# Splitting the first weight load of a two-problem GQA kernel, and reordering its first matmuls around the two pieces

## The chip, the cores and the metric

The kernel runs on one core of a Trainium2 chip. The metric is device time in microseconds (us) from one launch.

Names used below: PE is TensorE, PEld its weight loads, DVE is VectorE, ACT is ScalarE, SP is the sync engine, which here issues almost all DMA loads. SPq or PEq in a profile is the sequencer of that engine, which waits and issues. Lnnn is a line of the kernel; lines after L485 are up to four higher in the changed kernel.

## The reference

Two independent problems A and B, each a block of grouped-query attention with cached keys and values; their outputs are put side by side.

```python
# per problem: x (16, 32, 1024), k/v cache (16, 4, 512, 128), wq (1024, 4096), wo (4096, 1024), bf16
q = (x @ wq).reshape(16, 32, 32, 128).transpose(0, 2, 1, 3)
k = jnp.repeat(k_cache, 8, axis=1); v = jnp.repeat(v_cache, 8, axis=1)
p = softmax(einsum("bhqd,bhkd->bhqk", q, k) * 128 ** -0.5)
o = einsum("bhqk,bhkd->bhqd", p, v).transpose(0, 2, 1, 3).reshape(16, 32, 4096) @ wo
```

## The kernel before

The program has a head and a long main loop. The head projects the first 8 query heads of problem A (`first_heads`), 8 chunks of 128 along the model dimension by 8 heads, into 8 accumulators that fill PSUM. Then 128 slots of attention follow (128 pairs of batch and key head); in each slot 7 (in every fourth 6) "units", that is background matmuls, are mixed in: the projections of all other heads of A, then those of B, then the output projections. This mixing keeps PE full.

The head, with cuts:

```python
NF = REP - 2          # 6 heads start first; REP = 8
HC = DC // 2          # DC = 8 chunks of the model dimension, TT = 4 blocks of 128 tokens
...
load_x(0, 0, TT // 2)             # tokens, chunks 0 and 1, first half of the tokens: 128 KB
load_w0(0, 1, 0, NF)              # weights of chunk 0, heads 0..5: 192 KB, rows of 1,536 bytes
load_x(0, TT // 2, TT)            # the other token half: 128 KB
load_w0(1, 2, 0, NF)              # weights of chunk 1: 192 KB
load_x(2, 0, TT)                  # tokens, chunks 2 and 3: 256 KB  ("second-chunk tokens" below)
load_w0(2, 3, 0, NF)
load_w0(3, 4, 0, NF)
load_w0(0, HC, NF, REP)           # heads 6 and 7, chunks 0..3: 256 KB
load_w0(HC, HC + 2, 0, REP)       # 512 KB
load_x_transposed(HC)             # tokens, chunks 4 and 5, transposed by the DMA: 256 KB
load_w0(HC + 2, DC, 0, REP)
load_x_transposed(HC + 2)
load_wq(0, 2)                     # weights of heads 8..11: 1 MB, the first of the streamed projections
load_k(0)
...
warm_up(22)                       # 128-column matmuls on constants, result not used
transpose_x(0, 0, TT // 2)        # PE transposes, then DVE copies one chunk and ACT the other
warm_up(2)
first_heads(range(0, NF // 2), (0,), 0, TT // 2)
transpose_x(0, TT // 2, TT)
first_heads(range(NF // 2, NF), (0,), 0, TT // 2)
first_heads(range(NF), (0,), TT // 2, TT)
first_heads(range(0, NF // 2), (1,))
transpose_x(2, 0, TT)             # the "second transposes"
first_heads(range(NF // 2, NF), (1,))
first_heads(range(NF), (2, 3))
...                               # heads 6 and 7, then chunks 4..7; results leave PSUM
```

The loads of the main loop are issued by SP from a plan, slot by slot. SP issues them in this one order, and each waits there for its buffer to be free:

```python
at(GRP * (j - 1) - 2, load_k, j)                            # keys, 4 slots' worth
at(GRP * (j - 1) + 2, load_v, j, 2 if j < 4 else 1)         # values
at(max(0, int(need) - 10), load_wq, c4 // 8, c4 % 8)        # 1 MB of projection weights
for n, (d0, d1) in enumerate(((0, 2), (2, 5), (5, DC))):    # tokens of problem B, DMA-transposed,
    at(GRP * (n + 4) - 2, load_xT_b, d0, d1)                # in three parts: slots 14, 18, 22
```

## Time and profile before

| | kernel before |
|---|---|
| time, median | 344.55 us (343.79 to 344.85, 3 executions) |
| span of the profiled execution | 342.3 us |
| PE busy | 335.6 us, 98% |
| first head matmul | 4.50 us |
| second transposes begin | 7.65 us |
| hand-over: first matmul of the streamed projection | 19.98 us |
| last output matmul starts | 338.94 us |

Two parts of the page of the kernel before, busy time by engine and the chain of waits that ended last:

```profile
PE 335.6 (98%) x2087; PEld 214.1 (63%) x2126; DVE 266.5 (78%) x336; ACT 186.1 (54%) x209; POOL 47.1 (14%) x206
PE 96%; DMA 1%; issue 1%; SPq 1%; ACT 0%; ACTq 0%
```

The timeline of PE in the head shows where it stands still. Columns: start in us, time to the end of the group in us (ends are modelled, so groups overlap), engine, line, operation, output and inputs, count, and in brackets idle time before it and what ended it.

```profile
3.24 0.63 PE L521 MATMUL xT_ps<-ident,x_sb 128*128 128x128 bf16 x4
3.67 0.42 PE L513 MATMUL q_ps<-const-bfloat16-1.0 128*128 128x128 bf16 x2
4.50 0.82 PE L531 MATMUL q_ps<-xT,w_sb 128*128 128x256 bf16 x3 [0.41 <-DMA w_sb<-in_A_wq_dram]
5.11 0.63 PE L521 MATMUL xT_ps<-ident,x_sb 128*128 128x128 bf16 x4
5.54 1.89 PE L531 MATMUL q_ps<-xT,w_sb 128*128 128x256 bf16 x12
7.65 0.62 PE L521 MATMUL xT_ps<-ident,x_sb 128*128 128x128 bf16 x8 [0.22 <-DMA x_sb<-in_A_x_dram]
8.33 11.82 PE L531 MATMUL q_ps<-xT,w_sb 128*128 128x512 bf16 x53
19.98 1.24 PE L302 MATMUL q_ps<-xT,wq_sb 128*128 128x512 bf16 x5
...
```

The brackets count from the modelled end of the matmul before. Measured from start to start, less what a matmul of that size takes in a dense stream (107 ns per 128 columns at first, later 56, 109 and 216 ns for 128, 256 and 512), PE lost 0.62 us before 4.50 us and 0.38 us before 7.65 us. All waits given below are counted in that second way. The 0.22 us hole before 8.33 us is a dropped record: its weight load is there.

### The profile page before, as it was taken

The page shows a single profiled execution, that of the slowest core. Times are in us where ns is not written, and L with a number is a line of the kernel's source. Part 1 is how long each engine was busy: PE and PEld are TensorE (multiplying, and loading weights), DVE is VectorE, ACT ScalarE, POOL GpSimd, SP SyncE. Part 2 cuts the span into 40 slices and gives each one's busy share as a digit, 9 for nine tenths or more (in the row PEclk, how much of TensorE's full clock was granted, in tenths as well). Part 3 has the DMA queues.
Part 4 walks back from the last instruction along what each step waited for, and adds up shares of the span by engine and source line. Part 5 has one row for each costly group of instructions (what it writes and reads, how often), then busy time and mean ns, then how long its engine had stood idle before and what let it go on. Part 6 is the DMA issues. An engine that isn't in the chain of part 4 may idle for free.

```text
span 342.3 us, 5465 instructions
## 1 busy us (share of the span) xinstructions
PE 335.6 (98%) x2087; PEld 214.1 (63%) x2126; DVE 266.5 (78%) x336; ACT 186.1 (54%) x209; POOL 47.1 (14%) x206
## 2 busy tenths in 40 slices
PE   8999999999999999999999999999999999999996
PEld 6456666666666666666666666666666666666555
DVE  1057988888889888988888888888988888888540
ACT  2067666676676666666655455555455445555010
POOL 0001111100111111111101112222122110111100
PEclk9999999999999999999999999999999999999999
DMA  6988999999899999999999457998449985440001
GB/s 186 313 218 192 334 249 262 259 213 243 243 255 251 273 247 241 223 254 285 261 333 279 138 124 194 291 313 223 117 119 300 333 188 139 105 112 0 17 17 33
DMA packets 126958, 71.70 MB, mean 209 GB/s; under 512 B 75857, under 2 KB 126161, under 8 KB 126929
## 3 DMA queue, kind: packets, MB, share of 16 engines
q1 hardware_dynamic: 126400, 70.21, 84.4%
q0 software_dynamic: 384, 1.05, 0.9%
q8 instruction: 17, 0.28, 0.3%
q14 instruction: 13, 0.10, 0.1%
q10 hardware_dynamic: 144, 0.07, 0.1%
HBM read 50.86 MB, written 2.10 MB: 155 GB/s over the span
## 4 chain that ended last, share of the span: by engine, by line
PE 96%; DMA 1%; issue 1%; SPq 1%; ACT 0%; ACTq 0%
PE f_ps L321 32%; PE q_ps L302 28%; PE ob L426 17%; PE s_ps L358 16%; PE q_ps L531 3%; DMA x_sb<-in_A_x_dram 1%; SPq L478 0%; SPq L466 0%; PE xT_ps L521 0%; ACT o_sb L330 0%; SPq L701 0%; ACTq L330 0%
## 5 line engine op out<-in xcount | busy, mean ns | idle before, releaser
L366 ACT ACTIVATE p_sb<-s_ps,shift 128x1024 bf16<-128x1024 f32 x128 | 142.7, 1115 | 100.0 <-PE s_ps L358 85.7
L377 DVE TRANSPOSE_TENSOR_REDUCE parts<-p_sb 128x32 f32<-128x1024 bf16 x128 | 158.9, 1241 | 19.4 <-ACT p_sb L366 17.9
L321 PE MATMUL f_ps<-wo_sb,oT 128*128 128x512 bf16 (+1 forms) x525 | 127.5, 366 | 0.6
L302 PE MATMUL q_ps<-xT,wq_sb 128*128 128x512 bf16 x430 | 113.7, 379 | 0.6
L426 PE MATMUL ob<-p_sb,v_sb 128*128 128x256 bf16 x512 | 76.8, 273 | 0.8
L358 PE MATMUL s_ps<-qT,kT 128*128 128x256 bf16 x512 | 76.8, 273 | 0.0
L321 PEld LDWEIGHTS <-oT 128*128 128x128 bf16 x544 | 53.2, 98 | 36.0
L358 PEld LDWEIGHTS <-kT 128*128 128x128 bf16 x512 | 56.8, 113 | 28.4 <-issue 0.3
L302 PEld LDWEIGHTS <-wq_sb 128*128 128x128 bf16 x448 | 43.8, 98 | 31.5
L426 PEld LDWEIGHTS <-v_sb 128*128 128x128 bf16 x512 | 50.1, 98 | 20.0
L448 DVE TENSOR_TENSOR oT<-r,ob 128x512 bf16<-128x512 f32 x64 | 44.0, 687 | 22.5 <-PE ob L426 22.0
L412 DVE STREAM_TRANSPOSE r<-rall 128x512 f32<-128x512 f32 x64 | 44.2, 691 | 1.1
L310 ACT CAST qT<-q_ps 128x512 bf16<-128x512 f32 x56 | 32.7, 583 | 13.8 <-PE q_ps L302 13.8
L395 POOL COPY half<-cs 64x32 f32<-64x32 f32 x32 | 6.6, 206 | 228.1 <-DVE cs L385 228.1
L330 ACT CAST o_sb<-f_ps 128x512 bf16<-128x512 f32 (+1 forms) x17 | 9.5, 559 | 24.4 <-PE f_ps L321 16.7
L531 PE MATMUL q_ps<-xT,w_sb 128*128 128x512 bf16 (+1 forms) x68 | 14.5, 368 | 0.5 <-DMA w_sb<-in_A_wq_dram 0.4
L385 DVE TENSOR_REDUCE cs<-parts 128x32 f32<-128x128 f32 x32 | 12.0, 376 | 1.1
L407 DVE RECIPROCAL rall<-sums 128x32 f32<-128x32 f32 x32 | 10.5, 329 | 1.7 <-POOL sums L404 1.6
L531 PEld LDWEIGHTS <-w_sb 128*128 128x128 bf16 x70 | 6.9, 101 | 7.2 <-DMA w_sb<-in_A_wq_dram 0.7
L556 DVE CAST qT<-q_ps 128x512 bf16<-128x512 f32 x4 | 2.8, 692 | 9.6 <-PE q_ps L531 9.5
L332 POOL DMA_DIRECT2D out_dram<-o_sb x8 | 4.6, 575 | 33.1 <-ACT o_sb L330 33.1
L396 POOL TENSOR_TENSOR half<-half,cs 64x32 f32<-64x32 f32 x32 | 7.8, 245 | 2.6
(25 smaller groups left out, 46.2 us busy)
## 6 DMA issues: line engine op xcount, KB each, us to landing
wq_sb<-in_B_wq_dram SPq DMA_DIRECT2D x8, 1024.0 KB, 6.5
wo_sb<-in_A_wo_dram SPq DMA_DIRECT2D x8, 1024.0 KB, 6.5
v_sb<-in_B_v_cache_dram SPq DMA_DIRECT2D x16, 512.0 KB, 4.5
wo_sb<-in_B_wo_dram SPq DMA_DIRECT2D x8, 1024.0 KB, 8.8
v_sb<-in_A_v_cache_dram SPq DMA_DIRECT2D x14, 512.0 KB, 6.1
wq_sb<-in_A_wq_dram SPq DMA_DIRECT2D x6, 1024.0 KB, 5.9
w_sb<-in_A_wq_dram SPq DMA_DIRECT2D x2, 512.0 KB, 5.6
kT<-in_A_k_cache_dram SPq DMA_TRANSPOSE x64, 4.4
```

The source lines that it names most:

```text
L302: nc.tensor.matmul(ps[:], lhsT=w[:, dc, (h % 4) * DH:(h % 4 + 1) * DH], rhs=xT[pr][:, dc, :], start=(dc == 0), stop=(dc == DC - 1),)
L310: nc.scalar.copy(out=qT[pr, g][:, :, hl, :], in_=ps[:].rearrange("p (b s) -> p b s", s=SQ),)
L321: nc.tensor.matmul(ps[:, 0:width], lhsT=oT[pr, tt][:, h, :], rhs=wo_tiles[pr, nh, h // REP][:, h % REP, off:off + width], start=(h == 0), ...
L358: nc.tensor.matmul(s_ps[:, c, :], lhsT=kT[:, i % GRP, c, :], rhs=qT[pr, g][:, b, :, :].rearrange("p h s -> p (h s)"), start=True, stop=True,)
L366: nc.scalar.activation(out=p_sb[:], in_=s_ps[:], func=ACTF.Exp, bias=shift[:], scale=SCALE)
L377: nc.vector.tensor_reduce(out=parts[k][:, q, :, :].rearrange("p c h -> p (c h)"), in_=st[i]["p"][:].rearrange("p c (h s) -> p (c h) s", s=SQ),
L385: nc.vector.tensor_reduce(out=cs[:], in_=parts.pop(k)[:].rearrange("p q c h -> p q h c"), axis=AX.X, op=ALU.add,)
L407: nc.vector.reciprocal(out=rall[:, k, :], in_=quad.pop(k)[:])
L412: nc.vector.transpose(out=r[:].rearrange("p n s -> p (n s)"), in_=rall[:, k, o * 2 * REP:(o + 1) * 2 * REP] .unsqueeze(2).to_broadcast([P, ...
L426: nc.tensor.matmul(ob[j][:, q, :], lhsT=v_sb[:, i % GRP, c, :], rhs=st[i]["p"][:, c, :], start=(c == 0), stop=(c == KC - 1),)
L448: nc.vector.tensor_tensor(out=out, in0=rcp.pop(j)[:].rearrange("p (q h) s -> p q h s", h=REP), in1=ob.pop(j)[:].rearrange("p q (h s) -> p ...
L531: nc.tensor.matmul(first_q[h][:, ts], lhsT=w0[dc // HC][:, dc % HC, h * DH:(h + 1) * DH], rhs=xT[0][:, dc, ts], start=(dc == 0 and t0 == 0 ...
```

## The change

It has three parts. The 192 KB load of chunk 0's weights becomes two loads of 96 KB (heads 0 to 2, then heads 3 to 5, with the second token half between), so that PE can start on three heads sooner. The matmuls are reordered to suit, three heads over both token halves, then the other three; one more head of chunk 1 stands before the second transposes, and there are two warm-up matmuls more. One value load of the main loop is no longer split, which brings the number of loads back to what it was.

```diff
             load_x(0, 0, TT // 2)
-            load_w0(0, 1, 0, NF)
+            load_w0(0, 1, 0, NF // 2)
             load_x(0, TT // 2, TT)
+            load_w0(0, 1, NF // 2, NF)
             load_w0(1, 2, 0, NF)
...
             transpose_x(0, 0, TT // 2)
-            warm_up(2)
-            first_heads(range(0, NF // 2), (0,), 0, TT // 2)
+            warm_up(3)
+            first_heads((0, 1), (0,), 0, TT // 2)
             transpose_x(0, TT // 2, TT)
-            first_heads(range(NF // 2, NF), (0,), 0, TT // 2)
-            first_heads(range(NF), (0,), TT // 2, TT)
-            first_heads(range(0, NF // 2), (1,))
+            first_heads((2,), (0,), 0, TT // 2)
+            warm_up(1)
+            first_heads((0, 1, 2), (0,), TT // 2, TT)
+            first_heads((3, 4, 5), (0,), 0, TT // 2)
+            first_heads((3, 4, 5), (0,), TT // 2, TT)
+            first_heads(range(0, NF - 2), (1,))
             transpose_x(2, 0, TT)
-            first_heads(range(NF // 2, NF), (1,))
+            first_heads(range(NF - 2, NF), (1,))
...
-                at(GRP * (j - 1) + 2, load_v, j, 2 if j < 4 else 1)
+                at(GRP * (j - 1) + 2, load_v, j, 2 if j < 3 else 1)
```

## The prediction

> **What bounds it now.** TensorE. The page's busy table gives PE 335.6 of 342.3 us (98%), and the chain of waits is 96% PE. In the list of single matmuls, every gap after 8.1 us is one dropped record (215 ns, its weight load present): from the second group of token transposes at 7.65 us to 339.2 us PE streams without a pause, at 216 ns per 512-column matmul. So only the head can win time. There PE stands still twice: 0.62 us from 3.88 us (last warm-up matmul) to 4.50 us, waiting for the 192 KB of first-chunk weights, whose last of 16 engine landings is at 4.45 us; and 0.38 us from 7.27 to 7.65 us, waiting for the 256 KB of second-chunk tokens, last landing 7.61 us, though 14 of 16 had landed by 6.4 us. One 512-byte packet there took 1.3 us, so this wait is partly luck of the run. Together 1.0 us.
>
> **What the change does.**
> 1. It halves the first weight load. Three heads' 96 KB should land near 4.0 us (estimate: the first engine of the 192 KB load was done at 3.47 us, a packet of 1,536 B took 65 ns). The first matmul then waits for the DVE copy of the tokens (ends 3.99 us) and starts near 4.05 us: 0.45 us earlier. The second token half is no longer behind the other 96 KB and should land near 4.5 instead of 4.85 us.
> 2. It adds two warm-up matmuls (107 ns each in this stage), one filling a wait for a copy. The heads' matmuls are the same, reordered.
> 3. The clock takes most of item 1 back. Matmuls start every 107 ns for 128 columns until 5.73 us and every 56 ns after. The Trainium skill, "TensorE: Matmul & The Clock Gate", Part 1, says the array runs at half rate until a window of activity has passed; this trace agrees, with its step at 5.73 us, 4.8 us after the first matmul. Work moved before that step is done at half speed, so 0.45 us earlier is worth about 0.2 us, less one warm-up.
> 4. One more second-chunk matmul (0.216 us) stands before the second transposes. If their tokens still land at 7.6 us, PE waits there 0.2 us instead of 0.38 and the gain is just that matmul, 0.2 us. If the tokens come early (no straggler), my sum gives 0.1 to 0.2 us.
> 5. It adds one DMA issue (0.45 us of SP) ahead of these tokens: they may land up to 0.2 us later and cancel the gain. Later first-chunk loads have 0.4 to 3 us of slack and hold. One later value load is no longer split; that changes nothing.
>
> **Sum:** 0.0 to 0.4 us won, all on the critical path and kept to the end. Three runs of before differ by 1.06 us, so this is inside the noise.
>
> Predicted: 344.3 us, 8 in 10 between 343.5 and 344.9. Faster by over 2%: 0.005; within 2%: 0.99; slower: 0.005.
>
> **What would show it.** Item 1: first head matmul at 4.0 to 4.1 us. Item 3: the rate step still near 5.7 us. Items 4 and 5: second transposes still begin when their tokens land, 7.5 to 7.8 us. Then the first score matmul moves from 21.06 us to about 20.85 us, and the gaps after it are unchanged.
>
> **What would make it wrong.** The clock step moving by a microsecond; a straggling DMA engine in either profile; 768-byte packets being much slower per byte; a load in the main loop coming late.

## The result, and the profile after

The changed kernel took 344.41 us (median of 6 executions, 343.94 to 345.55); the kernel before took 344.55 us (6 executions, 343.79 to 344.94). The ratio is 1.0002, with a 95% interval of 0.9982 to 1.0022. Ratios here are the mean time of one kernel's runs over that of the other's in the same rounds, so not quite the ratio of the medians. Executions over 1.5% slower than the fastest of the same kernel are left out of the means. No difference can be told.

The profiled execution had a span of 342.9 us, 0.6 us longer than before's. The same two parts of its page:

```profile
PE 338.1 (99%) x2128; PEld 214.3 (63%) x2128; DVE 266.4 (78%) x336; ACT 186.1 (54%) x209; POOL 47.0 (14%) x206
PE 92%; DMA 4%; SPq 3%; issue 0%; ACT 0%; ACTq 0%
```

PE's busy time rose mainly because fewer matmul records were dropped (2,128 against 2,087). The chain has changed more than the time: DMA and SP's queue have 7% of it instead of 2%. PE's timeline in the head of the changed kernel:

```profile
3.24 0.63 PE L522 MATMUL xT_ps<-ident,x_sb 128*128 128x128 bf16 x4
3.67 0.53 PE L514 MATMUL q_ps<-const-bfloat16-1.0 128*128 128x128 bf16 x3
4.04 0.59 PE L532 MATMUL q_ps<-xT,w_sb 128*128 128x256 bf16 x2
4.42 0.63 PE L522 MATMUL xT_ps<-ident,x_sb 128*128 128x128 bf16 x4
...
7.15 0.61 PE L522 MATMUL xT_ps<-ident,x_sb 128*128 128x128 bf16 x8
7.60 5.17 PE L532 MATMUL q_ps<-xT,w_sb 128*128 128x512 bf16 x22
13.34 7.07 PE L532 MATMUL q_ps<-xT,w_sb 128*128 128x512 bf16 x32 [0.57 <-DMA xT<-in_A_x_dram]
20.24 1.24 PE L302 MATMUL q_ps<-xT,wq_sb 128*128 128x512 bf16 x5
```

The first head matmul starts at 4.04 us, 0.46 us earlier. The second transposes start at 7.15 us, 0.50 us earlier and with one more matmul already done: PE is 0.7 us ahead. Then it loses all of it. It waits 0.22 us at 10.4 us, for the weights of heads 6 and 7 (inside the group that starts at 7.60 us), and 0.73 us before 13.34 us, for the DMA-transposed tokens of chunks 4 and 5. The hand-over comes at 20.24 us, 0.26 us later than before. There is a further wait at 86 us. The chain of waits of the changed kernel in that stretch; columns are start, length and what:

```profile
79.71 6.47 DMA xT<-in_B_x_dram
86.18 0.04 issue
86.22 1.02 PE q_ps L302 x4
```

The last part of problem B's tokens landed at 86.18 us and PE, which needed it, had waited 0.32 us. In the trace before it landed at 84.41 us and was first used at 85.65 us. PE's timeline at this place shows it, first before, where the six matmuls run through:

```profile
85.21 1.46 PE L302 MATMUL q_ps<-xT,wq_sb 128*128 128x512 bf16 x6
```

and then in the changed kernel, where the third of them waits:

```profile
85.47 0.59 PE L302 MATMUL q_ps<-xT,wq_sb 128*128 128x512 bf16 x2
86.22 1.02 PE L302 MATMUL q_ps<-xT,wq_sb 128*128 128x512 bf16 x4 [0.16 <-DMA xT<-in_B_x_dram]
```

So the trace says: the first 7 us were won, and the loads behind them took the win back. One trace of each kernel can't tell whether that is a property of the change or of two executions.

### The profile page after: what moved, and what is told of

It is laid out like the page before. It is cut to its first block, busy times and chain, and to the rows that moved or that the text cites. A ratio compares the mean times of both kernels' runs of the same rounds, so it can differ in the third digit from the quotient of the medians.

```text
span 342.9 us, 5510 instructions
## 1 busy us (share of the span) xinstructions
PE 338.1 (99%) x2128; PEld 214.3 (63%) x2128; DVE 266.4 (78%) x336; ACT 186.1 (54%) x209; POOL 47.0 (14%) x206
## 4 chain that ended last, share of the span: by engine, by line
PE 92%; DMA 4%; SPq 3%; issue 0%; ACT 0%; ACTq 0%
PE f_ps L321 32%; PE q_ps L302 26%; PE s_ps L358 16%; PE ob L426 16%; DMA xT<-in_A_x_dram 2%; PE q_ps L532 2%; DMA xT<-in_B_x_dram 2%; SPq L276 1%; SPq L478 1%; SPq L466 0%; SPq L246 0%; ACT o_sb L330 0%; SPq L287 0%; SPq L705 0%; ACTq L330 0%
## 5 line engine op out<-in xcount | busy, mean ns | idle before, releaser
L377 DVE TRANSPOSE_TENSOR_REDUCE parts<-p_sb 128x32 f32<-128x1024 bf16 x128 | 158.9, 1241 | 19.8 <-ACT p_sb L366 18.3
L321 PE MATMUL f_ps<-wo_sb,oT 128*128 128x512 bf16 (+1 forms) x544 | 131.8, 366 | 0.0
L302 PE MATMUL q_ps<-xT,wq_sb 128*128 128x512 bf16 x448 | 117.7, 379 | 0.2 <-DMA xT<-in_B_x_dram 0.2
L532 PE MATMUL q_ps<-xT,w_sb 128*128 128x512 bf16 (+1 forms) x70 | 15.2, 368 | 0.6 <-DMA xT<-in_A_x_dram 0.6
L407 DVE RECIPROCAL rall<-sums 128x32 f32<-128x32 f32 x32 | 10.4, 325 | 1.6 <-POOL sums L404 1.6
L560 DVE CAST qT<-q_ps 128x512 bf16<-128x512 f32 x4 | 2.8, 692 | 10.4 <-PE q_ps L532 10.3
```

The source lines that it names most:

```text
L302: nc.tensor.matmul(ps[:], lhsT=w[:, dc, (h % 4) * DH:(h % 4 + 1) * DH], rhs=xT[pr][:, dc, :], start=(dc == 0), stop=(dc == DC - 1),)
L321: nc.tensor.matmul(ps[:, 0:width], lhsT=oT[pr, tt][:, h, :], rhs=wo_tiles[pr, nh, h // REP][:, h % REP, off:off + width], start=(h == 0), ...
L377: nc.vector.tensor_reduce(out=parts[k][:, q, :, :].rearrange("p c h -> p (c h)"), in_=st[i]["p"][:].rearrange("p c (h s) -> p (c h) s", s=SQ),
L407: nc.vector.reciprocal(out=rall[:, k, :], in_=quad.pop(k)[:])
L532: nc.tensor.matmul(first_q[h][:, ts], lhsT=w0[dc // HC][:, dc % HC, h * DH:(h + 1) * DH], rhs=xT[0][:, dc, ts], start=(dc == 0 and t0 == 0 ...
```

## The experiments

Two theories stand at the start. Theory Q: the load queue is a floor of its own; PE cannot be ahead of it, so time won in the head turns into waits at 10 to 14 us or at 86 us. Theory L: those waits were the luck of one execution.

The runs are told in three groups. This table has what each trace showed. "Step" is where the profile's record of the granted clock goes to full rate. The landing of a load is the last of its 16 completion events. "Last" is the start of the last output matmul. All in us.

| trace | step | first head matmul | second-chunk tokens land | A tokens 4, 5 land | streamed weights land | hand-over H | B tokens land, X | last |
|---|---|---|---|---|---|---|---|---|
| before | 5.73 | 4.50 | 7.61 | 11.84 | 18.76 | 19.98 | 84.41 | 338.94 |
| b1_before_again | 5.81 | 4.51 | 8.24 | 12.36 | 19.50 | 20.61 | 86.97 | 340.31 |
| after | 5.43 | 4.04 | 6.98 | 13.29 | 19.99 | 20.24 | 86.18 | 339.51 |
| a1_after_again | 3.58 | 4.04 | 6.97 | 12.68 | 20.03 | 20.08 | 85.43 | 339.04 |
| loadonly | 5.25 | 4.09 | 7.18 | 12.63 | 19.30 | 20.19 | 86.61 | 339.95 |
| orderonly | 5.91 | 4.45 | 7.45 | 12.18 | 19.14 | 19.82 | 85.86 | 339.19 |
| xb_before | 6.57 | 4.36 | 8.80 | 12.92 | 19.71 | 21.17 | 75.48 | 340.13 |
| xb_before2 | 5.93 | 4.51 | 7.12 | 12.29 | 20.12 | 20.16 | 76.61 | 339.29 |
| xb_after | 5.59 | 4.04 | 7.11 | 12.22 | 18.92 | 19.35 | 73.81 | 338.31 |
| xb_after2 | 4.30 | 4.14 | 7.06 | 12.26 | 19.16 | 19.29 | 75.47 | 338.24 |
| xb_act | 6.34 | 4.50 | 7.40 | 12.02 | 19.30 | 19.96 | 75.80 | 338.91 |
| xb_pad | 6.83 | 4.41 | 7.38 | 13.04 | 20.13 | 20.18 | 76.14 | 339.15 |
| xlate_before | 5.20 | 4.52 | 6.95 | 11.47 | 19.27 | 19.45 | 92.45 | 348.16 |
| xlate_after | 5.55 | 4.04 | 7.30 | 12.80 | 19.50 | 19.75 | 93.36 | 348.80 |

### Group 1: both kernels again, and each half of the change alone

**a1_after_again** and **b1_before_again** are the two kernels unaltered, for second traces.

> The changed kernel unaltered, for a second trace. In the first trace TensorE was 0.51 us ahead at the second transposes (7.15 against 7.65 us with one matmul more behind it), then waited 0.22 us at 10.4 us and 0.73 us at 12.4 us for late loads, and the hand-over (first matmul of the streamed projection) came at 20.24 us, against 19.98 in before. Theory Q (the loads after 8 us are a floor of their own): again waits of 0.3 to 0.9 us between 10 and 14 us, hand-over 19.7 to 20.3. Theory L (luck of one execution): waits under 0.15 us, hand-over 19.2 to 19.5. Time the same as before within 0.2% either way.

Measured: 344.10 us (median of 4), ratio to before 0.9965 (0.9916 to 1.0015). PE waited 0.85 us in all before the second transposes (0.51 us for copies of transposed tokens, 0.34 us for the weights of chunk 1), 0.40 us before 12.72 us for the A tokens, 0.45 us before the hand-over for the 1 MB of streamed weights, which landed at 20.03 us. Hand-over 20.08 us. That is theory Q's forecast, and L's (19.2 to 19.5) is out for this trace. The forecast of the time, the same within 0.2%, can't be tested with so wide an interval. The eleven executions of the kernel before and of b1 in this job have a mean 0.86 us above these four (standard error 0.32 us). It also has a useful accident: the clock reached full rate at 3.58 us instead of 5.43 us, so each matmul of the head was twice as fast for nearly 2 us, and still the second transposes began at 7.10 against 7.15 us and the hand-over at 20.08 against 20.24 us. What PE could have won by the faster clock went into waits for copies and loads.

> The kernel before unaltered, for a second trace and for the noise of one trace. Theory Q: the loads land within 0.5 us of the first trace (tokens by DMA transpose at 11.8 us), since they are paced by the queue; hand-over 19.7 to 20.1. Theory L: landings after 8 us scatter by over 1 us between traces of the same kernel. Ratio 1.000 with an interval that shows how small a difference these runs can tell.

Measured: 344.90 us (median of 4), ratio 0.9982 (0.9931 to 1.0034). The second-chunk tokens landed at 8.24 us and PE waited 0.98 us for them; hand-over 20.61 us, out of Q's range; tokens by DMA transpose at 12.36 us, 0.52 us later than in the first trace. So the landings do scatter from execution to execution, as L says, and PE follows them, as Q says. At 86 us this execution of the kernel *before* waited 0.74 us, more than the changed one had:

```profile
76.81 1.26 SPq L276
78.06 0.04 issue
78.11 1.26 SPq L276
79.37 0.04 issue
79.41 0.58 SPq L246
79.99 0.04 issue
80.04 6.93 DMA xT<-in_B_x_dram
86.97 0.04 issue
87.02 1.02 PE q_ps L302 x4
```

This is its chain of waits in order of time. Key loads (L276) and a 1 MB weight load (L246) are issued by SP just ahead of the B tokens; the tokens are issued at 80.04 us and land 6.93 us later.

**loadonly** is before with the split load (and the unsplit value load), in before's order of matmuls.

```diff
-            load_w0(0, 1, 0, NF)
+            load_w0(0, 1, 0, NF // 2)
             load_x(0, TT // 2, TT)
+            load_w0(0, 1, NF // 2, NF)
```

> Before with the split weight load alone (and the unsplit later value load), matmul order as in before. First head matmul at 4.0 to 4.1 us instead of 4.50; the first chunk's other three heads must not wait. Theory Q: any gain is eaten by waits at 10 to 14 us or at 85 us. If the extra issue and smaller packets delay the queue, the DMA-transposed tokens land 0.3 us or more after 11.8 us; if not, within 0.3 us. Hand-over 19.4 to 20.2.

Measured: ratio 1.0024 (0.9968 to 1.0079). First head matmul 4.09 us, as expected. PE then waited 0.28 us at 6.4 us, 0.13 us at 7.2 us and 0.63 us at 8.9 us for the weights of chunks 1 and 2 and the second-chunk tokens, and 0.80 us at 86 us. The tokens by DMA transpose came 0.79 us later than in the first trace of before. Hand-over 20.19 us.

**orderonly** has the changed order and warm-ups, with the load in one piece (and the value load split as before).

> The changed order of matmuls and the four warm-ups, with the weight load in one piece. First head matmul waits for the whole 192 KB: 4.4 to 4.6 us. At the second transposes one more matmul is done: gain of 0.1 to 0.2 us over before there if the tokens land late, a loss of up to 0.15 us if not. Tokens by DMA transpose at 11.5 to 12.2 us, as in before. Hand-over 19.7 to 20.0 under both theories.

Measured: ratio 0.9987 (0.9936 to 1.0038). First head matmul 4.45 us; second transposes 7.61 us; hand-over 19.82 us; A tokens at 12.18 us; these are within what was expected. It waited 0.41 us at 86 us.

What the six traces say together: the waits move about. In four of the six PE waited at 86 us, and there the last output matmul starts 253.33 us after the landing X (253.33 in each of the four). In the other two it starts 318.96 and 318.97 us after the hand-over H. So

last output matmul = the later of H + 318.96 us and X + 253.33 us.

This is a far better reading than "PE is 98% busy". There are two floors, and the matmuls of the head move only one of them. The other is set by the queue: in all six traces SP issues load after load, at most 0.12 us apart, from 20 us until it has issued the B tokens, and X differs by 2.56 us between two traces of the same kernel (84.41 and 86.97 us). An X of 85.9 us counts as much as an H of 20.3 us (X less 65.63 us).

### Group 2: the second floor moved away, and moved in

**xb_before** and **xb_after** are the two kernels with one more edit: the last part of B's tokens is issued a slot earlier, ahead of a value, a key and a 1 MB weight load.

```diff
-                at(GRP * (n + 4) - 2, load_xT_b, d0, d1)
+                at((14, 18, 21)[n], load_xT_b, d0, d1)
```

> Before, with one edit: the last third of the second problem's tokens (a DMA transpose) is issued one slot earlier, ahead of a value, a key and a 1 MB weight load. In 4 of 6 traces so far (2 of 3 with this kernel's head loads) TensorE stood still at 85 to 87 us until that load landed, for 0.3 to 0.8 us, and the last output matmul then started 253.33 us after the landing in all four. Theory Q (the load queue is a second floor): the load lands by 82 us, no wait at 85 to 87 us, the last output matmul starts at hand-over plus 318.96 us, mean time 0.2 to 0.6 us under before and a smaller spread. Theory L (the waits are only traces' luck): no difference in time, ratio 1.000.

> The changed kernel with the same edit as xb_before. Theory Q, head included: waits at 10 to 14 us or for the streamed weights at 19 to 20 us remain, hand-over 19.8 to 20.3 us as before, so the time equals xb_before within 0.15%. If instead only the wait at 86 us had hidden the change's gain, hand-over near 19.5 us and the time is 0.3 to 0.6 us under xb_before.

**xb_before2** and **xb_after2** repeat them.

> Repeat of xb_before, for a second trace and more times. The last output matmul starts at hand-over plus 318.96 us within 0.03, no wait at 85 to 87 us. Second-chunk tokens (one piece of first weights) land after 7.4 us and hold TensorE, as in the traces with that load in one piece: 7.61, 8.24, 7.45, 8.80 us. Hand-over 19.9 to 21.2 us.

> Repeat of xb_after. Second-chunk tokens land before 7.3 us (6.98, 6.97, 7.18, 7.11 so far with the split load). Hand-over 19.3 to 20.3 us, last output matmul 318.96 us later. If the change pays once the wait at 86 us is gone, the mean is 0.3 to 0.9 us under xb_before2, as the mean hand-overs so far (19.89 against 20.59 us) say; if the changed head only moves its waits to later loads, the two are equal within 0.2 us.

Measured, 6 executions each:

| | mean, us | median, us | ratio to the kernel before, same rounds |
|---|---|---|---|
| xb_before | 344.39 | 344.24 | 0.9993 (0.9966 to 1.0021) |
| xb_before2 | 344.31 | 344.34 | 0.9989 (0.9969 to 1.0009) |
| xb_after | 343.76 | 343.79 | 0.9982 (0.9958 to 1.0006) |
| xb_after2 | 343.76 | 343.73 | 0.9976 (0.9958 to 0.9994) |

The B tokens landed at 73.8 to 76.6 us, about 10 us earlier, and no trace has a wait at 86 us. The last output matmul starts at H + 318.96 us in three of the four, within 0.01; in xb_before2 it is 0.17 us later, because PE waited 0.15 us for a value load at 31.6 us. That one missed its expectation, and so did its second-chunk tokens, which landed at 7.12 us and not after 7.4 us; what held its hand-over at 20.16 us was the 1 MB of streamed weights, landed at 20.12 us.

xb_before was to be 0.2 to 0.6 us faster than before, with a smaller spread; that is not shown. Its twelve executions in two jobs are 0.15 us below the kernel before in the mean (standard error 0.24 us), which fits theory L's "no difference" as well. In the traced execution its head was the later of its two floors (H of 21.17 us, with the second-chunk tokens at 8.80 us). xb_after was expected by theory Q to keep its waits at 10 to 14 us and an H of 19.8 to 20.3 us; instead it shows H of 19.35 and 19.29 us and no such wait, so Q's claim that the *head* is always paced by its loads is wrong, and the alternative written beside it fits: with the wait at 86 us gone, the changed head is worth something. Pooled over the two jobs, xb_after's 12 executions have a mean of 343.76 us and xb_before's 344.35 us, ratio 0.9983. Standard errors from the scatter of the executions are 0.08 and 0.18 us, so the difference of 0.59 us is about three times its own (0.20 us); it is 0.63 us in one job and 0.55 us in the other. The traces point the same way, but do not show it alone: over five traces each of the two heads (before, b1, xb_before, xb_before2, xlate_before, against after, a1, xb_after, xb_after2, xlate_after) the mean hand-over is 20.28 and 19.74 us, 0.54 us apart, with a standard error of 0.35 us from their scatter.

What the four runs do not show is that the wait at 86 us hides the gain in the kernels as they stand. The same sum for the unedited pair over its two jobs (ten executions of the changed kernel, seventeen of before with b1) gives a mean 0.44 us lower for the changed kernel, with a standard error of 0.26 us: +0.06 us in the first job and -0.86 us in the second. The gain with the edit (0.59 us) and without it (0.44 us) can't be told apart.

PE's waits in xb_after, over the whole execution, are none but the start:

```profile
engine line waited for: us in total, times, longest us
PE q_ps L514 <- PEq L694: 0.9, 1, 0.9
```

This is the list of who waited for whom, filtered to PE; it leaves out waits under 0.15 us. In its head PE runs through from the second transposes to the hand-over, where the changed kernel stood still before 13.34 us:

```profile
7.67 11.84 PE L532 MATMUL q_ps<-xT,w_sb 128*128 128x512 bf16 x53
19.35 1.24 PE L302 MATMUL q_ps<-xT,wq_sb 128*128 128x512 bf16 x5
```

The changed kernel's list of waits had two lines more:

```profile
PE q_ps L532 <- DMA xT<-in_A_x_dram: 0.6, 1, 0.6
PE q_ps L302 <- DMA xT<-in_B_x_dram: 0.2, 1, 0.2
```

**xlate_before** and **xlate_after** are the opposite: the B tokens are issued later, in slot 26, to make the second floor so high that nothing in the head can matter.

```diff
-                at(GRP * (n + 4) - 2, load_xT_b, d0, d1)
+                at((14, 18, 26)[n], load_xT_b, d0, d1)
```

> Before, with the last third of the second problem's tokens issued one slot group later instead: behind a value, four keys and a 1 MB weight load more. Two-floor theory: it lands near 95 us (85.4 estimated from the first five traces plus 10), TensorE waits 8 to 11 us at 86 us, and the last output matmul starts 253.33 us (within 0.1) after that landing: time 352 to 356 us. If the end follows the hand-over alone, no change.

> The changed kernel with the same later load. Two-floor theory: whatever the head won is swallowed by the wait at 86 us; end is again landing plus 253.33 us, and its time differs from xlate_before by as much as the two landings differ, under 0.3% and not with the hand-over. If TensorE's head were the bound, it would still be ahead or behind by the difference of the hand-overs.

Measured: 354.48 and 353.17 us (medians of 4; ratios to before 1.0287 and 1.0239). PE waited 7.4 and 8.0 us at 85 us. Between the two traces the landing X is 0.91 us later in xlate_after, the hand-over 0.30 us later, the last output matmul 0.64 us later. The landings came 1.6 to 2.6 us sooner than expected and the wait a little shorter; the times are in the stated range. The formula missed: the last output matmul starts 255.7 and 255.4 us after the landing, not 253.33. What adds the 2.4 and 2.1 us is the clock. Stretches of xlate_after, with columns: stretch in us, its length, busy us and count of PE, PEld, DVE, ACT and POOL, granted clock, DMA share, GB/s:

```profile
80.00:85.00 5.00, 5.00 (x34) 3.33 (x34) 3.89 (x5) 3.82 (x5) 0.00 (x0) 1.00 0.98 301
85.00:93.00 8.00, 0.52 (x3) 0.18 (x2) 2.94 (x5) 0.64 (x1) 1.30 (x6) 0.87 1.13 270
93.00:98.00 5.00, 4.60 (x16) 2.25 (x16) 0.69 (x1) 1.70 (x2) 0.00 (x0) 0.53 0.90 195
98.00:103.00 5.00, 5.00 (x33) 3.13 (x31) 3.07 (x5) 2.83 (x4) 0.00 (x0) 1.00 0.62 205
```

The granted clock falls to half in the idle stretch and comes back at 97.71 us, 4.35 us after the landing; half of 4.35 is 2.2 us. (In xlate_before: at 97.36 us, 4.91 us after, half is 2.5.) In both traces it fell 5.4 to 5.5 us after PE's last matmul. The Trainium skill, "TensorE: Matmul & The Clock Gate", section "HAM oscillation — how this bites in real kernels", says that a wait of over about 3.4 us brings the half rate back; these two waits agree.

The two kernels' executions differ by 0.3% in the mean (354.23 and 353.16 us, a difference of 1.07 us with a standard error of 0.51 us), at the edge of what was expected and in the opposite sense to the two traced landings. Untraced executions do not show their landings, so whether the changed kernel's loads come earlier by a microsecond on average at this place, or four executions are too few, stays open.

### Group 3: what about the split steadies the second-chunk tokens?

One thing nobody expected stands in the table. The second-chunk tokens are issued 0.48 us later in the changed kernel and land earlier: at 6.97 to 7.30 us in six traces with the split (after, a1, loadonly, xb_after, xb_after2, xlate_after), mean 7.10, against 6.95 to 8.80 us in six with one piece (before, b1, orderonly, xb_before, xb_before2, xlate_before), mean 7.70. The scatter of six traces gives this difference of 0.60 us a standard error of 0.29 us, so chance is not excluded. Two runs looked for a reason.

**xb_act** is xb_after with the second piece issued by ACT, so that SP issues no load more than before.

```diff
-            load_w0(0, 1, NF // 2, NF)
+            load_w0(0, 1, NF // 2, NF, nc.scalar)
```

> As xb_after, but the second half of the split weight load is issued by ACT, so SP issues as many loads as in before. In three traces with the split the first DMA-transposed tokens landed at 12.6 to 13.3 us, in three without it at 11.8 to 12.4 us. Theory issue (SP's extra 0.48 us delays everything behind it): they land at 11.8 to 12.3 us here and the hand-over comes 0.3 to 0.5 us earlier than in xb_after. Theory engines (the DMA engines are the limit, whoever issues): 12.6 us or later, hand-over unchanged.

Measured: mean 344.23 us, ratio 0.9995 (0.9970 to 1.0020). A tokens at 12.02 us, as theory "issue" had it, but so nearly had xb_after (12.22 us), and the hand-over was later, 19.96 against 19.35 us. The piece issued by ACT landed at 2.96 to 3.34 us, before everything else; the first tokens landed at 3.68 instead of 3.06 to 3.32 us, and the first head matmul started at 4.50 us. This agrees with what the Trainium skill says in "DMA: Bandwidth & Descriptors", section "Issuing engines are not separate DMA queues": a load issued by another engine interleaves on the same DMA engines. It tells nothing about the issue cost, because it changed the order too. Its second-chunk tokens landed at 7.40 us, later than in any of the six traces with the split issued by SP, and its mean is 0.47 us above xb_after's in the same job (standard error 0.22 us): as far as one trace goes, this speaks against a split in any order being enough.

**xb_pad** is xb_before with one more, 4 KB load issued at the place of the second piece: the later issue without the split.

```diff
             load_x(0, TT // 2, TT)
+            pad = const.tile([P, 16], BF16, name="pad")
+            nc.sync.dma_start(out=pad[:], in_=wq_v[:, 0, 0:16])
             load_w0(1, 2, 0, NF)
```

> xb_before with the first weights in one piece, but one more load issued (4 KB, unused) where the changed kernel issues its second half: the loads behind it are issued 0.48 us later, as in the changed kernel. Second-chunk tokens landed at 6.95 to 8.80 us (mean 7.70) in six traces with one piece, at 6.97 to 7.30 (mean 7.10) in six with two. If the later issue alone steadied them: here before 7.3 us, time like xb_after (343.8 us). If the smaller pieces did it: scattered, time like xb_before (344.3 us). First weights 4.3 to 4.5 us, second token half 4.7 to 4.9 us in any case. One trace within 6.95 to 7.3 us settles nothing by itself; the times then decide.

Measured: mean 344.57 us, ratio 1.0000 (0.9983 to 1.0017): like xb_before (344.35 us), not like xb_after. Second-chunk tokens at 7.38 us; first weights at 4.36 us and second token half at 4.77 us, as expected. So, as far as times from another job and one trace can say, a later issue alone does not do it. The split in this order, with the second token half between its pieces, remains, and so does chance; by what mechanism it would steady a load three places behind it was not shown. All this stays open.

## Why the prediction was right or wrong

The number was right: 344.3 us forecast, 344.41 us measured, within the noise as said. But the stated range, 343.5 to 344.9 us, holds anything from no gain to a gain of 1 us, so the number would have come out right for many mechanisms; that it did is in part luck. Of the steps that led to it some held and some failed, in opposite senses. The first score matmul, forecast at 20.85 us, came at 21.32 us.

- **First head matmul at 4.0 to 4.1 us: right.** 4.04 us in four traces of the changed kernel and its variants with SP issuing both pieces, 4.14 us in xb_after2 and 4.09 us in loadonly. The 96 KB landed at 3.6 us, earlier than the estimate of 4.0 us; the DVE copy was then the limit, as the prediction said.
- **"The clock takes most of item 1 back": not the limit.** The arithmetic is sound, but the step is not at 5.7 us. It lay between 3.58 and 6.83 us in fourteen traces. The trace with the earliest step (a1, 3.58 us) won nothing by it, since PE then waited for copies and loads: the lead of the head was set by landings more than by the clock.
- **"It adds one DMA issue (0.45 us of SP) ahead of these tokens: they may land up to 0.2 us later": wrong in sign.** They landed 0.6 us earlier (6.98 against 7.61 us; means of six traces each 7.10 and 7.70 us). The second transposes began at 7.15 us, not at 7.5 to 7.8 us as stated. This term was mis-sized by 0.6 to 0.8 us, against the change; how much of that is chance stays open (Group 3).
- **"Later first-chunk loads have 0.4 to 3 us of slack and hold": wrong for the traced execution.** In the changed kernel's trace the weights of heads 6 and 7 landed at 10.82 us instead of 9.56, the A tokens at 13.29 instead of 11.84, and PE waited 0.96 us in all. Had they landed as in before, PE, which was ready for them at 10.64 and 12.60 us, would not have waited: the later landings did it, not PE's lead. For the A tokens the extra issue may have a part in it: they landed at 12.70 us in the mean of the seven traces in which SP has one issue more ahead of them (xb_pad among them) and at 12.15 us in the other seven (xb_act among them), 0.55 us apart with a standard error of 0.23 us. Slack read from one trace was less than the scatter between traces: A tokens landed at 11.5 to 13.3 us.
- **"all on the critical path and kept to the end": wrong, and this is the step that mattered.** Slack at 86 us in before's trace was 1.24 us, which the prediction did not look at: it took the absence of waits in one trace for the absence of a floor. In four of the six traces of kernels with that load in its old place, the end was set by the landing of B's tokens, 253.33 us before the last output matmul starts, whatever the head had done. A head that is 0.5 us earlier (20.28 to 19.74 us in the mean) need not show in the time then. With that load out of the way the same head was worth 0.59 us, 0.17%, with a standard error of 0.20 us.

So the gain, expected at 0.0 to 0.4 us, came out at 0.59 us (standard error 0.20 us) with the second floor out of the way. In the first trace of the changed kernel it was lost already in the head, to the 0.96 us of waits at 10 to 14 us, and 0.32 us more went at 86 us. How much of it survives on average in the changed kernel as it stands can't be told from times: the interval of its ratio, 0.9982 to 1.0022, holds both nothing and 0.17%, and the job with a1 even favours the changed kernel (0.9965, 0.9916 to 1.0015). That the second floor can take the gain is shown by the traces, in which the end follows X; that it is what hid the gain in the times is not shown.

The version that combines the change with the earlier B tokens (xb_after) ran at 343.76 us in the mean, twice, 0.2% below the kernel before (ratios 0.9982 and 0.9976). It is the best of all runs here, by little. It was never timed in the same job as the changed kernel itself, whose ten executions in two other jobs have a mean of 344.34 us. The unsplit value load was not tried by itself.

## What to carry to other kernels

When one engine is 98% busy, look for loads that landed just in time, not only for those that were waited for: list landing against first use for each, over several traces, and treat a slack below the scatter as a floor. A gain ahead of such a floor can disappear without leaving a wait in every trace; a formula such as "end = landing + constant" in several traces is the sign. Moving one queued load by one slot may then be the other half of the optimization; here the pair of edits came out 0.2% below the kernel before, and what the moved load adds to the change is not shown apart.

## What the Trainium skill lacked or had wrong

- "TensorE: Matmul & The Clock Gate", Part 1, "What you observe", puts the step to full rate "around 4µs into sustained matmul activity, ±500ns run-to-run". That it is not tied to the kernel's start, as the same part says, agrees with the runs; but in fourteen traces it came 2.7 to 5.9 us after the first matmul (at 0.93 us), a spread of 3.2 us, though PE also stood still for up to 0.6 us in that stretch. The ±500 ns is too narrow for these kernels; a note further down in the same part does call the count of slow matmuls run-variable.
- "DMA: Bandwidth & Descriptors", "Specifications", gives about 27 GiB/s per engine and 512 B as the least transfer for line rate. In the head of before a 512 B packet took 27 ns in the median (19 GB/s), a 1,536 B packet 65 ns (24 GB/s) and a 2,048 B packet 84 ns (24 GB/s): at 512 B the median packet still moves some 20% less per ns than the longer ones. By the mean packet (29, 85 and 86 ns) 512 and 1,536 B are alike, near 18 GB/s, and only 2,048 B is better.
- The same page's rules, "Rules for kernel authors", advise to coalesce small transfers and say that under 64 KB overhead dominates. They have no word on what a first load delays. Here 192 KB in one piece landed at 4.31 to 4.48 us in six traces and held the 128 KB behind it to 4.69 to 4.88 us; in two pieces, with those 128 KB between, with SP issuing both, they landed at about 3.6, 4.1 and 4.8 to 5.0 us.
- The same page, "DMA Transpose (X-bar)", has no word on how a DMA transpose and the loads around it land. In the head the completion events of the early loads were spread (2.1 us from first to last for before's second-chunk tokens), and those of the first transpose and of the four loads behind it lay within 0.1 to 0.3 us. So, before, did those of the load just ahead of it (10.80 to 10.86 us), so it isn't shown that the transpose does it. In the changed kernel's trace 17 packets of 256 B that began between 10 and 12 us took over 0.3 us each, 22 us together (before: 9, 5 us together). The cause was not looked for.
- None of the pages read gives the scatter of a load's landing from one execution to the next. For the second-chunk tokens, with the first weights in one piece, it was 6.95 to 8.80 us in the traces here, more than the change was meant to win.
